# Windowed attention and spatial gating on one core: q and k transposed by identity products into f32 PSUM, batch 0 as a software pipeline, Ln directly behind its product, turns a batch ahead

## The chip, the cores and the metric

The kernel runs on one core of one Trainium2 chip. The metric is the device time of one launch in microseconds. A kernel is run several times; the text gives medians with the lowest and highest run. A run more than 1.5% above the fastest of the same kernel counts as slow, and comparisons use fast runs alone.

Names of engines in the profile: PE is TensorE, PEld its weight loads, DVE is VectorE, ACT is ScalarE, POOL is GpSimd, SP is SyncE. A "q" behind a name (ACTq) is that engine's sequencer, for instance where it issues a DMA.

## The reference

There are 8 batches of 8 heads, 576 positions and head size 64. The attention is causal with a window of 64 positions; its output goes through a gated block that mixes positions.

```python
scores = q @ k.T / sqrt(64);  mask = (0 <= rel) & (rel < 64)
attn   = softmax(where(mask, scores, -1e9));  x = attn @ v        # -> [8, 576, 512]
h = maximum(x @ w_in, 0);  u, v = h[..., :512], h[..., 512:]
v_n = (v - mean(v)) / sqrt(var(v) + 1e-6)
v_s = einsum('ts,bsd->btd', w_spatial, v_n) + b_spatial[None, :, None]
out = (u * v_s) @ w_out
```

All inputs and the output are f32 in memory; the kernel computes in f16 with f32 sums.

## The kernel before

Per batch the kernel treats five "pairs" `s`: four pairs of heads over the first 512 positions, and a fifth for the last 64 positions of all heads. A pair goes through T (transpose q and k), S (scores), E (Exp and mask), P (product with v and the row sums), N (normalise, giving x). The gated block of a batch consists of units V, L, U, G, O (products with w_in, the normalisation, the spatial product, w_out). The attention of batch a+1 is woven between the units of batch a.

Batches 0 to 3 (`NPE = 4`) transpose on PE. Each partition of a loaded tile holds four consecutive positions (`"(p t) d -> p (t d)"`, t=4), so the transposes come out sorted by t, and the copy home must interleave them: it writes every fourth f16.

```python
def emit_T(b, s):                                   # s < 4 shown
    tp = psp.tile([128, 1024], f16, tag="mm", bufs=4, ...)
    for y, x in enumerate("kq"):
        w = NH[b, x][:, 512 * s:512 * s + 512].rearrange("p (t n) -> p t n", t=4)
        for t in range(4):
            nc.tensor.transpose(tp[:, n * y + 128 * t:n * y + 128 * t + 128], w[:, t, :], id16[:, :])
    for y, x in enumerate("kq"):
        o = TR[b, x][:, :].rearrange("p (a n) -> p a n", a=4)
        nc.vector.tensor_copy(o[:, s, 0:512].rearrange("p (n t) -> p t n", t=4),
                              tp[:, n * y:n * y + n].rearrange("p (t n) -> p t n", t=4))
```

P writes the PSUM tile `oz`, of which there is only one buffer. N is in two halves: Ln of the row sums, then Exp of minus that and the multiply into x, which reads `oz` too. So the next P cannot start before x of the pair ahead is done.

```python
oz = psp.tile([128, 2, 512], f32, tag="oz", bufs=1, ...)              # in emit_P
# emit_N1: lnz = Ln(oz[:, 1])                       ScalarE
# emit_N2: zinv = Exp(-lnz)                         ScalarE
#          x = oz[:, 0] * zinv                      VectorE

def att(i, s):
    for f in state["post"]: f()
    post = []
    if s < 5:
        emit_S(i, s); emit_E(i, s)
    if state["P"] is not None:
        pb, ps_ = state["P"]
        emit_P(pb, ps_)
        post += [lambda: emit_N1(pb, ps_), lambda: emit_N2(pb, ps_)]
    state["P"] = (i, s) if s < 5 else None
    state["post"] = post
# run(a, seq): after every gated unit (V, U, G, O, L, W, Q):
#     if state["post"]: state["post"].pop(0)()
```

One entry of `post` is emitted after each following unit. Ln therefore stands behind the output of one unit and Exp and multiply behind the output of a second one. A unit O ends in a copy of its result on ScalarE and a store, which ScalarE issues for the first three batches:

```python
ob = mpool.tile([128, 512], f32, tag="ob", bufs=3, ...)
nc.scalar.copy(ob[:, :], po[:, :])
(nc.scalar if b < 3 else nc.sync).dma_start(out[b, 128 * j:128 * j + jn, :], ob[p0:p0 + jn, :])
```

Batch 0 has no batch ahead of it to weave into, and goes pair by pair, with matmuls on scratch data (`warm`) that are meant to keep PE's clock up:

```python
for s in range(4):
    ...                                             # casts of pair s+1, v, weights
    att(0, s)
    warm(4)
    emit_T(0, s + 1)
    warm(2)
```

The softmax here doesn't subtract the row's maximum and nothing guards it: scores larger than these inputs give would overflow.

## Time and profile before

| | before |
|---|---|
| time | 280.72 us (279.23 to 282.01, 3 runs) |
| span of the profiled run, granted clock | 280.1 us, 0.92 |
| busy PE / DVE / ACT | 80% / 64% / 54% |
| last x of batch 0, 1, 2, 3 ends at | 36.0, 77.0, 114.1, 149.2 us |
| copies of transposed k and q, 16 each | 1291 and 1337 ns |

The page of the profile gives busy time per engine, and below it the busy share of the 16 DMA engines in 40 equal slices of the span (a digit of 9 is 90% or more):

```profile
...
PE 223.3 (80%) x2733; PEld 118.7 (42%) x2733; DVE 178.1 (64%) x329; ACT 151.7 (54%) x272; POOL 110.1 (39%) x157
...
DMA  7999999999896903979031002899289922002104
...
```

No engine is full over the whole span. The DMA engines are close to full for about the first 80 us, in which batches 0 to 3 are loaded. From the groups of instructions (line, engine, operation, tiles, shapes, count, then busy us and mean ns, then idle time before them and what ended it):

```profile
...
L398 DVE TENSOR_TENSOR x<-oz,zi 128x512 f16<-128x512 f32 (+1 forms) x40 | 25.2, 631 | 39.9 <-ACT zi L396 39.6 <-issue 0.3
...
L268 DVE COPY tq<-tp 128x512 f16<-128x512 f16 x16 | 21.4, 1337 | 0.0
L268 DVE COPY tk<-tp 128x512 f16<-128x512 f16 x16 | 20.7, 1291 | 7.2 <-PE tp L258 7.2
...
```

The copies of line 268 take about twice as long as the multiply of line 398 (685 ns for its 128x512 form alone; the 631 above mixes in a smaller form), although both read and write 512 elements per partition. From the waits (engine, line and what it waited for, then us in total, times, longest):

```profile
...
PE oz L370 <- DVE x L398: 26.4, 22, 3.1
...
PE sc L286 <- DVE tq L268: 16.2, 8, 5.0
...
```

PE waits 26.4 us for x to free `oz`, and 16.2 us for the copies before it can start scores. The chain of waits that ended last, in order of time (start, duration, what), for one pair of batch 1:

```profile
...
60.24 1.83 PE po L528 x4
...
62.09 0.59 ACT ob L531
...
62.71 0.35 ACTq L441
...
63.11 0.60 ACT ln L388
63.71 0.48 ACT ob L531
...
64.22 0.34 ACTq L441
...
64.60 0.64 ACT zi L396
...
65.26 0.70 DVE x L398
...
66.00 0.64 PE oz L370 x2
...
```

This is the code of `att` and `run` at work. P has ended at 60.24; then come product, copy and store issue of a unit O (62.09, 62.71), and only then Ln (63.11); then copy and store of the next unit (63.71, 64.22), and only then Exp (64.60), the multiply on DVE (65.26), and the next P at 66.00. The same view for one transpose of batch 2:

```profile
...
90.59 0.46 PE tp L258 x8
...
91.08 1.31 DVE tk L268
```

Eight transposes take 0.46 us, 0.057 us apart; the copy behind them takes 1.31 us.

### The profile page before, as it was taken

To read this page: it belongs to the slowest core of one execution; us is meant where nothing else is said; L and a number is where in the kernel's file an instruction comes from. 1 tells how busy PE (TensorE), PEld (TensorE's weight loads), DVE (VectorE), ACT (ScalarE), POOL (GpSimd) and SP (SyncE) were. 2 spreads that over 40 slices of the span, in tenths; PEclk is the share of its full clock that TensorE was granted. 3 is DMA by queue.
4 is the path that set the end of the run, shared out by engine and by line. 5 is a ranking of instruction groups with operands and counts; after the bars stand their busy time and mean duration, and the time that the engine had idled before them with its cause. 6 is when DMAs were issued, how large, how long until landed. Compare 5 with 4: busy or idle time off the path is not lost.

```text
span 280.1 us, 6696 instructions
## 1 busy us (share of the span) xinstructions
PE 223.3 (80%) x2733; PEld 118.7 (42%) x2733; DVE 178.1 (64%) x329; ACT 151.7 (54%) x272; POOL 110.1 (39%) x157
## 2 busy tenths in 40 slices
PE   7367998975775875877969877979797979797994
PEld 2234435633333552434524543534453545353451
DVE  5865467982378970698808873765576657662750
ACT  2353554344562744575445864775477547755823
POOL 3683686008920089200980494036902680000000
PEclk9977797977797998899989997997999899999999
DMA  7999999999896903979031002899289922002104
GB/s 204 251 228 229 239 192 267 207 263 277 181 195 143 160 2 107 257 142 170 3 129 41 3 5 80 193 194 192 98 196 194 200 89 81 21 2 112 59 0 169
DMA packets 77647, 40.43 MB, mean 144 GB/s; under 512 B 44272, under 2 KB 73008, under 8 KB 77616
## 3 DMA queue, kind: packets, MB, share of 16 engines
q1 hardware_dynamic: 73424, 34.22, 58.1%
q0 software_dynamic: 2224, 2.24, 4.7%
q10 hardware_dynamic: 1968, 3.54, 3.8%
q8 instruction: 21, 0.34, 0.6%
q14 instruction: 10, 0.08, 0.1%
HBM read 32.79 MB, written 9.44 MB: 151 GB/s over the span
## 4 chain that ended last, share of the span: by engine, by line
PE 47%; DVE 35%; ACT 12%; issue 4%; ACTq 1%; POOL 0%; POOLq 0%
PE ps L509 9%; PE pv L422 8%; PE po L528 8%; DVE x L398 6%; DVE tq L268 5%; DVE tk L268 5%; PE oz L370 5%; DVE vn L479 4%; DVE st L431 4%; DVE g L512 4%; PE pu L489 3%; PE oz L380 3%; DVE e L354 3%; ACT e L344 3%; ACT zi L396 2%
## 5 line engine op out<-in xcount | busy, mean ns | idle before, releaser
L171 POOL CAST nk<-fk 128x512 f16<-128x512 f32 (+2 forms) x23 | 19.2, 835 | 101.8 <-PE tp L263 61.7
L344 ACT ACTIVATE e<-sc 128x1024 f16<-128x1024 f32 x32 | 32.8, 1026 | 41.5 <-PE sc L286 23.6
L398 DVE TENSOR_TENSOR x<-oz,zi 128x512 f16<-128x512 f32 (+1 forms) x40 | 25.2, 631 | 39.9 <-ACT zi L396 39.6
L171 POOL COPY vs<-vn 64x512 f16<-64x512 f16 (+1 forms) x56 | 43.5, 776 | 3.1
L509 PE MATMUL ps<-wspT,vn 128*128 128x512 f16 (+1 forms) x160 | 40.2, 401 | 0.0
L531 ACT COPY ob<-po 128x512 f32<-128x512 f32 x32 | 18.8, 586 | 34.6 <-PE po L528 34.1
L431 DVE BATCH_NORM_STATS2 st<-vs 128x6 f32<-128x512 f16 (+1 forms) x40 | 27.0, 674 | 14.7 <-ACT vs L429 14.7
L354 DVE TENSOR_TENSOR e<-e,mask 128x1024 f16<-128x1024 f16 x32 | 25.8, 806 | 15.6 <-ACT e L344 15.5
L422 PE MATMUL pv<-win,x 128*128 128x512 f16 (+1 forms) x132 | 34.9, 412 | 0.0
L528 PE MATMUL po<-wout,g 128*128 128x512 f16 x128 | 34.7, 420 | 0.0
L489 PE MATMUL pu<-x,win 128*128 128x512 f16 x128 | 30.8, 391 | 0.0
L171 POOL CAST vn<-vf 128x512 f16<-128x512 f32 (+1 forms) x40 | 25.3, 640 | 10.9 <-DMA vf<-in_v_dram 10.1
L429 ACT ACTIVATE vs<-pv 128x512 f16<-128x512 f32 (+1 forms) x40 | 22.9, 597 | 8.2 <-PE pv L422 5.8
L388 ACT ACTIVATE ln<-oz 128x512 f32<-128x512 f32 (+1 forms) x40 | 22.1, 554 | 9.1 <-PE oz L380 6.6
L370 PE MATMUL oz<-e,onesK 128*64 128x512 f16 x64 | 14.2, 431 | 16.1 <-DVE x L398 15.8
L512 DVE TENSOR_TENSOR g<-ps,ru 128x512 f16<-128x512 f32 x32 | 21.6, 686 | 8.3 <-PE ps L509 8.1
L268 DVE COPY tk<-tp 128x512 f16<-128x512 f16 x16 | 20.7, 1291 | 7.2 <-PE tp L258 7.2
L396 ACT ACTIVATE zi<-ln 128x512 f32<-128x512 f32 (+1 forms) x40 | 23.5, 588 | 2.8 <-ACT ob L531 2.1
L509 PEld LDWEIGHTS <-vn 128*128 128x128 f16 (+1 forms) x160 | 15.3, 103 | 17.7 <-issue 3.7
L268 DVE COPY tq<-tp 128x512 f16<-128x512 f16 x16 | 21.4, 1337 | 0.0
L370 PEld LDWEIGHTS <-onesK 128*64 128x64 f16 x80 | 7.0, 109 | 31.3 <-issue 28.6
L171 POOL CAST nq<-fq 128x512 f16<-128x512 f32 (+2 forms) x23 | 18.7, 815 | 3.9 <-DMA fq<-in_q_dram 3.9
(82 smaller groups left out, 326.9 us busy)
## 6 DMA issues: line engine op xcount, KB each, us to landing
vf<-in_v_dram SPq DMA_DIRECT2D x40, 128.0 KB, 5.5
out_dram<-ob SPq DMA_DIRECT2D x20, 256.0 KB, 2.0
fk<-in_k_dram SPq DMA_DIRECT2D x32, 144.0 KB, 3.7
fq<-in_q_dram SPq DMA_DIRECT2D x32, 144.0 KB, 4.5
fk<-in_k_dram SPq DMA_DIRECT2D x16, 256.0 KB, 5.7
fq<-in_q_dram SPq DMA_DIRECT2D x16, 256.0 KB, 5.4
vf<-in_v_dram SPq DMA_DIRECT2D x16, 256.0 KB, 6.0
out_dram<-ob ACTq DMA_DIRECT2D x12, 256.0 KB, 2.8
```

The costliest lines, as they stand in the source:

```text
L171: nc.gpsimd.tensor_copy(o, i)
L268: nc.vector.tensor_copy(o[:, s, 0:512].rearrange("p (n t) -> p t n", t=4), tp[:, n * y:n * y + n].rearrange("p (t n) -> p t n", t=4))
L344: nc.scalar.activation(e2[:, :, :], sc[0][:, :, :], AF.Exp, bias=0.0, scale=0.125)
L354: nc.vector.tensor_tensor(e2[:, :, :], e2[:, :, :], m, ALU.min)
L370: nc.tensor.matmul(oz[64 * h:64 * h + 64, 1, 0:n], onesK[:, :], e2[:, h, 0:n], start=True, stop=True)
L398: nc.vector.tensor_tensor(x[:, 0:n], oz[:, 0, 0:n], zinv[:, 0:n], ALU.mult)
L422: nc.tensor.matmul(PV[b, j][0:jn, :], xcol(b, r, j), w_in_sb[:, r, 512:1024], start=(r == 0), stop=(r == 3))
L431: nc.vector.bn_stats(st6[0:jn, 0:6], vs[0:jn, :])
L489: nc.tensor.matmul(pu[:, :], w_in_sb[:, r, 128 * m:128 * m + 128], X[b, r][:, :], start=(r == 0), stop=(r == 3))
L509: nc.tensor.matmul(ps[:, :], VN[b, kk][0:kn, 128 * m:128 * m + 128], wspT[kk][0:kn, 0:512], start=(kk == 0), stop=(kk == 4))
L512: nc.vector.tensor_tensor(g[:, :], ps[:, :], ru[:, :], ALU.mult)
L528: nc.tensor.matmul(po[:, :], G[b, r][:, 128 * j:128 * j + 128], w_out_sb[:, r, :], start=(r == 0), stop=(r == 3))
```

## The change

The change does five things.

- (a) The four transposes of a pair become products with the identity into an f32 PSUM tile, and are written there with a stride of four elements, so that they lie in token order. The copy home becomes a contiguous cast. In batch 0 the copy of q goes to ScalarE.
- (b) Batch 0 becomes a software pipeline: mask and normalisation of earlier pairs stand between T and S of a pair; the casts of q go to POOL; two warm matmuls per pair disappear. The casts of a pair get a tile each.
- (c) Ln is emitted directly behind P, Exp and multiply behind the next unit.
- (d) Batches 5 to 7, which are turned by 32x32 blocks on DVE, are turned a batch ahead (`R` in place of `T`).
- (e) The casts on POOL are emitted a batch earlier, and the order of units changes a little.

```diff
-    def emit_T(b, s):
-        tp = psp.tile([128, 1024], f16, tag="mm", bufs=4, name=f"tp{b}_{s}")
+    def T_mm(b, s):
+            tp = [psp.tile([128, 512], f32, tag="mm", bufs=4, name=f"tp{b}_{s}{x}") for x in "kq"]
...
+                    o = tp[y][:, :].rearrange("p (n t) -> p t n", t=4)
                     for t in range(4):
-                        nc.tensor.transpose(tp[:, n * y + 128 * t:n * y + 128 * t + 128],
-                                            w[:, t, :], id16[:, :])
+                        nc.tensor.matmul(o[:, t, :], w[:, 128 * t:128 * t + 128], id16[:, :],
+                                         start=True, stop=True)
...
+    def T_out(b, s):
-                nc.vector.tensor_copy(o[:, s, 0:512].rearrange("p (n t) -> p t n", t=4),
-                                      tp[:, n * y:n * y + n].rearrange("p (t n) -> p t n", t=4))
+                (act_copy if b == 0 and y == 1 else dve_copy)(o[:, y, s, 0:512], tp[y][:, :])
...
@@ att @@
             emit_P(pb, ps_)
-            post += [lambda: emit_N1(pb, ps_), lambda: emit_N2(pb, ps_)]
+            emit_N1(pb, ps_)
+            post.append(lambda: emit_N2(pb, ps_))
...
@@ batch 0; emit_E split into E_exp and E_mask, emit_N2 into N_exp and N_mul @@
-    for s in range(4):
-        ...
-        att(0, s)
-        warm(4)
-        emit_T(0, s + 1)
-        warm(2)
+    for s in (0, 1, 2, 4, 3):
+        pairs_in(0, s, dve_copy, pool_copy if s != 3 else dve_copy)
+        if s == 4:
+            emit_T(0, 4)
+            continue
+        ...
+        T_mm(0, s)
+        if s > 0:
+            E_mask(0, s - 1)
+        if s > 1:
+            N_mul(0, s - 2)
+        T_out(0, s)
+        emit_S(0, s)
+        E_exp(0, s)
+        if s > 0:
+            emit_P(0, s - 1)
+            emit_N1(0, s - 1)
+            N_exp(0, s - 1)
         warm(4)
...
@@ batches 1 to 7: orders of units; two of the four @@
-            run(a, "V0 V1 V2 T0 V3 Q L U0 U1 A0 U2 T1 U3 U4 A1 G0 G1 A2 G2 G3 A3 G4 A4 O0 O1 O2 A5 O3")
+            run(a, "V0 V1 V2 V3 Q L T0 U0 U1 T1 A0 U2 U3 A1 U4 G0 G1 A2 G2 G3 A3 G4 O0 A4 R0 O1 O2 "
+                   "A5 R1 O3")
-            run(a, "T0 V0 V1 V2 A0 V3 Q A1 L U0 T1 U1 U2 U3 A2 U4 G0 G1 A3 G2 G3 G4 A4 O0 O1 O2 A5 O3")
+            run(a, "V0 V1 A0 V2 V3 Q A1 L U0 U1 U2 A2 U3 U4 G0 A3 G1 G2 G3 A4 G4 R0 O0 O1 A5 O2 R1 O3")
```

More of the change, by code (lines that the diff above doesn't have):

```diff
@@ L52 @@
     TR = {}
+    XI = {"k": 0, "q": 1}
     VF = {}
@@ L63, in new_qkv @@
             NF[b, x] = inpool.tile([128, 2560], f32, tag=f"f{x}", bufs=2, name=f"f{x}{b}")
-            NH[b, x] = inpool.tile([128, 2560], f16, tag=f"n{x}", bufs=1, name=f"n{x}{b}")
-            TR[b, x] = apool.tile([128, 2304], f16, tag=f"t{x}", bufs=2, name=f"t{x}{b}")
+            if b < NPE:
+                for s in range(5):
+                    NH[b, x, s] = inpool.tile([128, 512], f16, tag=f"n{x}{s}", bufs=1,
+                                              name=f"n{x}{s}_{b}")
+            else:
+                NH[b, x] = inpool.tile([128, 2304], f16, tag=f"n{x}", bufs=1, name=f"n{x}{b}")
+        TR[b] = apool.tile([128, 2, 2304], f16, tag="tr", bufs=2, name=f"tr{b}")
         VF[b] = inpool.tile([128, 5, 8, 64], f32, tag="vf", bufs=2, name=f"vf{b}")
@@ L84, in cast_four @@
         if s < 4:
-            copy(NH[b, x][:, 512 * s:512 * s + 512].rearrange("p (t h d) -> p h t d", t=4, h=2),
+            copy(NH[b, x, s][:, :].rearrange("p (t h d) -> p h t d", t=4, h=2),
                  NF[b, x][:, 512 * s:512 * s + 512].rearrange("p (h t d) -> p h t d", t=4, h=2))
         else:
-            copy(NH[b, x][0:64, 2048:2560], NF[b, x][0:64, 2048:2560])
+            copy(NH[b, x, 4][0:64, :], NF[b, x][0:64, 2048:2560])
     def load_pairs(b):
@@ L138, in turn @@
     def turn(b, x, hp):
-        o = TR[b, x][:, 1152 * hp:1152 * hp + 1152].bitcast(u32)
+        o = TR[b][:, XI[x], 1152 * hp:1152 * hp + 1152].bitcast(u32)
         n = NH[b, x][:, 1152 * hp:1152 * hp + 1152].bitcast(u32)
@@ L248 @@
     SC = {}
-    def emit_T(b, s):
-        tp = psp.tile([128, 1024], f16, tag="mm", bufs=4, name=f"tp{b}_{s}")
-        n = 512 if s < 4 else 256
+    TP = {}
+    def T_mm(b, s):
+        if s < 4:
+            tp = [psp.tile([128, 512], f32, tag="mm", bufs=4, name=f"tp{b}_{s}{x}") for x in "kq"]
+        else:
+            tp = psp.tile([128, 512], f16, tag="mm", bufs=4, name=f"tp{b}_{s}")
+        TP[b, s] = tp
         with nc.named_scope(f"T{b}_{s}"):
             for y, x in enumerate("kq"):
+                w = NH[b, x, s]
@@ L255, in emit_T @@
                 if s < 4:
-                    w = NH[b, x][:, 512 * s:512 * s + 512].rearrange("p (t n) -> p t n", t=4)
+                    o = tp[y][:, :].rearrange("p (n t) -> p t n", t=4)
                     for t in range(4):
-                        nc.tensor.transpose(tp[:, n * y + 128 * t:n * y + 128 * t + 128],
-                                            w[:, t, :], id16[:, :])
+                        nc.tensor.matmul(o[:, t, :], w[:, 128 * t:128 * t + 128], id16[:, :],
+                                         start=True, stop=True)
@@ L260, in emit_T @@
                 else:
-                    w = rest(NH[b, x])
                     for p in range(4):
-                        nc.tensor.transpose(tp[:, n * y + 64 * p:n * y + 64 * p + 64],
-                                            w[:, 2 * p:2 * p + 2, :], id16[0:64, 0:64])
-        for y, x in enumerate("kq"):
-            o = TR[b, x][:, :].rearrange("p (a n) -> p a n", a=4)
+                        nc.tensor.transpose(tp[:, 256 * y + 64 * p:256 * y + 64 * p + 64],
+                                            w[0:64, 128 * p:128 * p + 128], id16[0:64, 0:64])
@@ L267, in emit_T @@
+    def T_out(b, s):
+        tp = TP.pop((b, s))
+        o = TR[b][:, :, :].rearrange("p x (a n) -> p x a n", a=4)
+        for y in (0, 1):
             if s < 4:
-                nc.vector.tensor_copy(o[:, s, 0:512].rearrange("p (n t) -> p t n", t=4),
-                                      tp[:, n * y:n * y + n].rearrange("p (t n) -> p t n", t=4))
-            else:
-                nc.vector.tensor_copy(o[:, :, 512:576],
-                                      tp[:, n * y:n * y + n].rearrange("p (a n) -> p a n", a=4))
+                (act_copy if b == 0 and y == 1 else dve_copy)(o[:, y, s, 0:512], tp[y][:, :])
+            else:
+                nc.vector.tensor_copy(o[:, y, :, 512:576],
+                                      tp[:, 256 * y:256 * y + 256].rearrange("p (a n) -> p a n", a=4))
@@ L274, in emit_S_pe, with emit_T @@
+    def emit_T(b, s):
+        T_mm(b, s)
+        T_out(b, s)
     def emit_S_pe(b, s):
@@ L276, in emit_S_pe @@
         SC[b, s] = [sc]
-        K, Q = (TR[b, x][:, :].rearrange("p (a n) -> p a n", a=4) for x in "kq")
+        K, Q = (TR[b][:, y, :].rearrange("p (a n) -> p a n", a=4) for y in (0, 1))
         with nc.named_scope(f"S{b}_{s}"):
@@ L300, in scores @@
         rows = slice(32 * g, 32 * g + 32)
-        K, Q = (TR[b, x][:, :].rearrange("p (a n e) -> p a n e", a=2, e=2) for x in "kq")
+        K, Q = (TR[b][:, y, :].rearrange("p (a n e) -> p a n e", a=2, e=2) for y in (0, 1))
         return [lambda e=e: nc.tensor.matmul(
@@ L338, in emit_S, with E_exp @@
                             t[e]()
-    def emit_E(b, s):
+    def E_exp(b, s):
         sc = SC.pop((b, s))
@@ L344, in emit_E @@
             nc.scalar.activation(e2[:, :, :], sc[0][:, :, :], AF.Exp, bias=0.0, scale=0.125)
-            m = mask[:, :, :, :].rearrange("p h u w -> p h (u w)")
         else:
@@ L352, in emit_E, with E_mask @@
             nc.scalar.activation(e2[:, :, 0:n], sc[0][:, :, 0:n], AF.Exp, bias=0.0, scale=0.125)
+        E2[b, s] = e2
+    def E_mask(b, s):
+        e2 = E2[b, s]
+        if s < 4:
+            m = mask[:, :, :, :].rearrange("p h u w -> p h (u w)")
+        else:
             m = maskr[:, :, :].rearrange("p (h u) w -> p h (u w)", h=2)
         nc.vector.tensor_tensor(e2[:, :, :], e2[:, :, :], m, ALU.min)
-        E2[b, s] = e2
+    def emit_E(b, s):
+        E_exp(b, s)
+        E_mask(b, s)
     def slot(b, r):
@@ L389, in emit_N1, with N_exp, N_mul @@
         LZ[b, s] = lnz
-    def emit_N2(b, s):
+    ZI = {}
+    def N_exp(b, s):
         n = 512 if s < 4 else 256
         lnz = LZ.pop((b, s))
-        oz = OZ.pop((b, s))
         zinv = apool.tile([128, 512], f32, tag="zinv", bufs=2, name=f"zi{b}_{s}")
         nc.scalar.activation(zinv[:, 0:n], lnz[:, 0:n], AF.Exp, bias=0.0, scale=-1.0)
+        ZI[b, s] = zinv
+    def N_mul(b, s):
+        n = 512 if s < 4 else 256
+        zinv = ZI.pop((b, s))
+        oz = OZ.pop((b, s))
         x = xpool.tile([128, n], f16, tag=f"x{s}", bufs=2, name=f"x{b}_{s}")
@@ L399, in emit_N2 @@
         X[b, s] = x
+    def emit_N2(b, s):
+        N_exp(b, s)
+        N_mul(b, s)
     def mm(name):
@@ L573, in run @@
                         turn(a + 1, x, n)
+            elif c == "R":
+                if a + 2 < B:
+                    for x in "kq":
+                        turn(a + 2, x, n)
             elif c == "F":
@@ L617, in batch_in @@
                 shift_part(b, c // 2, pool_copy)
-    pairs_in(0, 0, dve_copy, act_copy)
-    v_in(0, 0)
-    emit_T(0, 0)
-    for s in range(4):
-        v_in(0, s + 1)
-        if s == 1:
+    for s in (0, 1, 2, 4, 3):
[3 more added lines that the diff above has]
+            continue
+        v_in(0, s)
+        if s == 2:
             load_win(1)
             load_win(0)
-        if s == 3:
-            load_wsp()
-            load_wout()
-        if s == 2:
-            pairs_in(0, 4, dve_copy, act_copy)
-        if s < 3:
-            pairs_in(0, s + 1, dve_copy, act_copy)
-        att(0, s)
+        T_mm(0, s)
[10 more added lines that the diff above has]
+            N_exp(0, s - 1)
         warm(4)
-        emit_T(0, s + 1)
-        warm(2)
+    v_in(0, 4)
+    load_wsp()
+    load_wout()
     load_pairs(2)
     batch_in(1)
-    att(0, 4)
-    run(0, "p0003 p0103 F")
-    att(0, 5)
-    run(0, "p0203 p0303 F p0034 o0 p0134 o1 p0234 o2 p0334 o3 Q L U0 U1 U2 U3")
+    emit_S(0, 4)
+    E_exp(0, 4)
+    E_mask(0, 3)
+    N_mul(0, 2)
+    run(0, "p0003 p0103")
+    emit_P(0, 3)
+    emit_N1(0, 3)
+    emit_N2(0, 3)
+    E_mask(0, 4)
+    run(0, "p0203 p0303")
+    emit_P(0, 4)
+    emit_N1(0, 4)
+    emit_N2(0, 4)
+    run(0, "p0034 o0 p0134 o1 p0234 o2 p0334 o3 Q L U0 U1 U2 U3")
     run(0, "W0 W1 W2 W3 W4 U4 T0 G0 G1 T1 A0 G2 G3 T2 A1 G4 O0 T3 A2 O1 O2 T4 A3 O3")
-    run(0, "A4 p1003 p1103 F A5 p1203 p1303 F")
+    run(0, "F A4 p1003 p1103 F A5 p1203 p1303 F")
     for a in range(1, B):
@@ L656 @@
                 load_batch(a + 2)
+        if a + 2 < B and a > 1:
+            batch_in(a + 2)
         if a == 1:
@@ L659 @@
                    "G1 G2 T4 A3 G3 G4 A4 O0 O1 A5 O2 O3")
+            batch_in(3)
         elif a == 2:
-            run(a, "V0 T0 V1 V2 T1 A0 V3 Q T2 A1 L U0 U1 U2 T3 A2 U3 U4 G0 G1 T4 A3 G2 G3 G4 A4 "
-                   "O0 O1 O2 A5 O3")
+            run(a, "V0 T0 V1 T1 A0 V2 V3 Q T2 A1 L U0 U1 U2 T3 A2 U3 U4 G0 T4 A3 G1 G2 G3 A4 "
+                   "G4 O0 O1 A5 O2 O3")
         elif a == 3:
-            run(a, "V0 V1 V2 T0 V3 Q L U0 U1 A0 U2 T1 U3 U4 A1 G0 G1 A2 G2 G3 A3 G4 A4 O0 O1 O2 A5 O3")
-        else:
-            run(a, "T0 V0 V1 V2 A0 V3 Q A1 L U0 T1 U1 U2 U3 A2 U4 G0 G1 A3 G2 G3 G4 A4 O0 O1 O2 A5 O3")
-        if a + 2 < B:
-            batch_in(a + 2)
+            run(a, "V0 V1 V2 V3 Q L T0 U0 U1 T1 A0 U2 U3 A1 U4 G0 G1 A2 G2 G3 A3 G4 O0 A4 R0 O1 O2 "
+                   "A5 R1 O3")
+        else:
+            run(a, "V0 V1 A0 V2 V3 Q A1 L U0 U1 U2 A2 U3 U4 G0 A3 G1 G2 G3 A4 G4 R0 O0 O1 A5 O2 R1 O3")
     run(B, "Q")
```

## The prediction

> **What bounds it now.** No engine is full: the page gives PE 80%, DVE 64%, ACT 54% of 280.1 us. The chain that ended last (47% PE, 35% DVE, 12% ACT) changes by stage; in order of time: batch 0's attention to its last x at 36.0 us; batch 0's V and normalisation to 44.8; batch 1's attention to 77.0; batch 2's to about 112; batch 3's to 145; then 31, 28, 28 and 26.5 us per batch, and a 21.7 us tail. In the stretches PE is busy 17 to 18 of 20 us late, about 15 of 20 before 145 us. There the chain goes through DVE copies of transposed q and k (5.2% + 4.9% = 28 us), which write f16 with a stride of four: 1291 and 1337 ns for 128x512, 1.1 us apart back to back. In batch 0 score groups start at 9.1, 13.7, 19.8, 26.8, 30.9 us although pair 3's v is in at 17.0; PE meanwhile runs its warm matmuls at 0.43 us each.
>
> **What changes.**
> 1. The stride moves from the DVE write to the PE write. The copy becomes contiguous f32 PSUM to f16. The Trainium skill (VectorE: DVE Perf Modes, "Why PSUM operands drop a tier") gives f32 from PSUM the 1x mode; the trace's f32-PSUM multiplies (685 ns, 0.6 apart) agree. Estimate 0.65 us, 0.58 apart: 32 copies save about 0.5 us of pitch each, four of batch 0 also go to ACT. About 18 us of DVE, 11 to 13 of it on the chain.
> 2. Identity products now write PSUM with a 16-byte stride. The Trainium skill (PSUM, "Specifications (TRN2)") says non-contiguous patterns slow matmuls significantly; no run here shows it yet. If halved in speed, 8 products of a pair go from 0.43 to 0.86 us: 7 us of PE in all, some 3 on the chain.
> 3. Batch 0 pipeline: mask and normalise of the previous pairs run between transpose and scores, q casts go to POOL, two warm matmuls per pair disappear. Scores of pair 3 come at about 20.5 instead of 26.8, x of batch 0 ends near 30.5 (the weights' arrival, issue at 14.3 plus 9.9 us, starts to bind): -5.5 us.
> 4. Ln directly behind P, no longer behind the next unit's output copy and store issue (chain at 60 to 72 us). About 1.4 us per affected step, two or three steps in batches 1 to 3: -4.
> 5. Batches 5 to 7 are turned a batch ahead, out of the chain (1.35 us per batch, PE waits of up to 2.4 us on it): about -1.5 per batch for four batches, -6.
>
> Per stage: batch 0 -5.5, batch 1 -5, batch 2 -4.5, batch 3 -3, later -5, minus 2 to 3 for the slower products: about -20 us.
>
> **Predicted 260 us, 250 to 270 for 8 in 10.** Faster by over 2%: 0.95; within 2%: 0.04; slower: 0.01.
>
> **Right if:** the copies show 0.6 to 0.7 us; DVE busy falls to about 158 us; x of batch 0 ends near 30 us; PE idle before "sc waiting for tq" (16 us) falls by half; the stretches after 145 us shorten by 1 to 2 us per batch. **Step wrong if:** identity products show over 0.3 us spacing, or PE waits for PSUM buffers behind them.
>
> **What would break it:** products slowed fourfold (+20 us of PE); DMA, full until 80 us, becoming the bound of batch 1 (its last v lands near 44 us); a lower granted clock (now 0.92) as PE gets denser; the gain of batch 0 given back waiting for w_in.

## The result, and the profile after

| | before | after |
|---|---|---|
| time | 281.37 us (279.23 to 283.40, 4 runs) | 260.98 us (258.21 to 263.23, 4 runs) |
| ratio of fast runs | | 0.920, 95% interval 0.907 to 0.933 |
| busy PE / DVE / ACT, us | 223.3 / 178.1 / 151.7 | 223.5 / 164.8 / 151.1 |
| last x of batch 0, 1, 2, 3 ends at | 36.0, 77.0, 114.1, 149.2 | 33.0, 72.1, 105.5, 132.6 |

All ratios here are the mean time of one kernel's fast runs over that of the other's fast runs of the same rounds, so not quite the ratio of the medians that stand beside them. Two of the four runs of after count as slow; its two fast ones have a mean of 258.8 us, against 281.3 of before. The profiled run of the changed kernel took 262.51 us and counts as slow (granted clock 0.93; its fast runs had 0.95 and 0.96), while that of the kernel before is fast. Readings that need exact sizes are therefore taken from the experiments, most of whose profiled runs are fast. The numerical result is correct here and in all runs below.

The page, same lines as before:

```profile
...
PE 223.5 (86%) x2725; PEld 120.6 (46%) x2725; DVE 164.8 (63%) x326; ACT 151.1 (58%) x271; POOL 115.0 (44%) x161
...
DMA  6999999999997903877086003899499932004105
...
```

PE does the same amount of work in a shorter span. The groups, for pair 2 (VectorE does k, and q except in batch 0; ScalarE does q of batch 0):

```profile
...
L180 DVE CAST tr<-tp_2k 128x512 f16<-128x512 f32 x4 | 2.7, 675 | 1.9 <-PE tp_2k L270 1.9
...
L180 DVE CAST tr<-tp_2q 128x512 f16<-128x512 f32 x3 | 2.0, 678 | 0.0
...
L183 ACT CAST tr<-tp_2q 128x512 f16<-128x512 f32 x1 | 0.6, 585 | 0.2 <-PE tp_2q L270 0.2
...
```

The contiguous copy takes 0.68 us on DVE in place of 1.29 to 1.34, and 0.59 us on ScalarE. The waits:

```profile
...
PE oz L396 <- DVE x L431: 15.8, 11, 3.1
...
PE sc L303 <- DVE tr L180: 6.2, 5, 2.3
...
```

Both waits of PE have shrunk, by 10.6 and 10.0 us. Identity products in the chain of waits, batch 2:

```profile
...
86.22 0.44 PE tp_2k L270 x4
86.65 0.44 PE tp_2q L270 x4
...
```

Four products now take 0.44 us, so 0.11 us apart: exactly half the speed of the transposes before. Finally, the timeline of ScalarE around the first stores of batch 0 (start, duration, instruction; in brackets how long it was idle before and what ended that):

```profile
...
52.22 0.59 ACT L414 ACTIVATE ln<-oz 128x512 f32<-128x512 f32 x1
52.84 0.63 ACT L423 ACTIVATE zi<-ln 128x512 f32<-128x512 f32 x1
53.45 0.58 ACT L568 COPY ob<-po 128x512 f32<-128x512 f32 x1
55.84 0.39 ACTq L478 DMA_DIRECT2D out_dram<-ob  x1
56.33 1.02 ACT L361 ACTIVATE e<-sc 128x1024 f16<-128x1024 f32 x1 [2.30 <-PE po L565]
...
```

Ln and Exp now stand together, and the copy `ob` has ended by 54.03. But its store is issued at 55.84, and ScalarE stood still for 1.8 us in between. This wait is new: in the kernel before, the first store was issued 0.03 us after its copy.

### The profile page after: what moved, and what is told of

It is laid out like the page before. It is cut to its first block, busy times and chain, and to the rows that moved or that the text cites. A ratio compares the mean times of both kernels' runs of the same rounds, so it can differ in the third digit from the quotient of the medians.

```text
span 260.8 us, 6702 instructions
## 1 busy us (share of the span) xinstructions
PE 223.5 (86%) x2725; PEld 120.6 (46%) x2725; DVE 164.8 (63%) x326; ACT 151.1 (58%) x271; POOL 115.0 (44%) x161
## 4 chain that ended last, share of the span: by engine, by line
PE 47%; SPq 17%; DVE 16%; ACT 9%; DMA 7%; issue 3%; ACTq 1%
PE ps L546 11%; PE pv L459 7%; PE po L565 7%; SPq L122 7%; SPq L83 7%; PE pu L526 6%; DMA vf<-in_v_dram 5%; DVE vn L516 5%; DVE st L468 4%; PE oz L396 3%; PE sc L319 3%; SPq L87 3%; DVE x L431 2%; PE oz L406 2%; ACT e L361 2%
## 5 line engine op out<-in xcount | busy, mean ns | idle before, releaser
L177 POOL COPY vs<-vn 64x512 f16<-64x512 f16 (+1 forms) x56 | 44.5, 794 | 3.1
L377 DVE TENSOR_TENSOR e<-e,mask 128x1024 f16<-128x1024 f16 x32 | 27.8, 868 | 21.3 <-ACT e L361 21.0
L546 PE MATMUL ps<-wspT,vn 128*128 128x512 f16 (+1 forms) x160 | 39.3, 394 | 0.0
L526 PE MATMUL pu<-x,win 128*128 128x512 f16 x128 | 34.3, 418 | 0.0
L565 PE MATMUL po<-wout,g 128*128 128x512 f16 x128 | 31.1, 385 | 0.0
L177 POOL CAST vn<-vf 128x512 f16<-128x512 f32 (+1 forms) x40 | 26.9, 682 | 9.1 <-DMA vf<-in_v_dram 8.3
L177 POOL CAST nq<-fq 128x512 f16<-128x512 f32 (+2 forms) x27 | 21.3, 790 | 12.8 <-DMA fq<-in_q_dram 10.9
L546 PEld LDWEIGHTS <-vn 128*128 128x128 f16 (+1 forms) x160 | 15.2, 102 | 16.7 <-issue 1.9
L528 ACT ACTIVATE ru<-pu 128x512 f32<-128x512 f32 x32 | 17.2, 593 | 6.0 <-PE pu L526 6.0
L459 PEld LDWEIGHTS <-x 128*128 128x128 f16 (+1 forms) x132 | 12.8, 104 | 16.1 <-issue 3.2
L526 PEld LDWEIGHTS <-win 128*128 128x128 f16 x128 | 12.2, 105 | 16.0 <-issue 5.5
```

The lines of the kernel that those rows point to most:

```text
L177: nc.gpsimd.tensor_copy(o, i)
L377: nc.vector.tensor_tensor(e2[:, :, :], e2[:, :, :], m, ALU.min)
L459: nc.tensor.matmul(PV[b, j][0:jn, :], xcol(b, r, j), w_in_sb[:, r, 512:1024], start=(r == 0), stop=(r == 3))
L526: nc.tensor.matmul(pu[:, :], w_in_sb[:, r, 128 * m:128 * m + 128], X[b, r][:, :], start=(r == 0), stop=(r == 3))
L546: nc.tensor.matmul(ps[:, :], VN[b, kk][0:kn, 128 * m:128 * m + 128], wspT[kk][0:kn, 0:512], start=(kk == 0), stop=(kk == 4))
L565: nc.tensor.matmul(po[:, :], G[b, r][:, 128 * j:128 * j + 128], w_out_sb[:, r, :], start=(r == 0), stop=(r == 3))
```

## The experiments

Twelve kernels were run in three calls, each beside its own runs of the kernel before (medians 281.26, 281.65 and 283.27 us; these differ between calls, so the ratios carry the comparison). A difference in us given below is one between means of fast runs; across calls it can be off by a us or two. "T" below is the new transposes with their copies, "N" is Ln directly behind P, "the pipeline" is batch 0's new order, "the turns" is the new unit orders with turns and casts a batch ahead.

| run | what it is | median us (range) | mean of fast runs (number) | ratio to before, 95% |
|---|---|---|---|---|
| after | T, N, pipeline, turns | 260.98 (258.21–263.23) | 258.8 (2) | 0.920 [0.907, 0.933] |
| only_T | before + T | 273.08 (272.40–273.15) | 272.9 (4) | 0.973 [0.969, 0.978] |
| only_TN | before + T + N | 259.59 (257.97–262.59) | 259.1 (3) | 0.915 [0.908, 0.922] |
| undo_T | after without T | 269.89 (269.68–270.72) | 270.0 (4) | 0.963 [0.958, 0.968] |
| read_stride | after, stride on the read of the copy | 260.80 (260.46–267.08) | 260.7 (3) | 0.929 [0.924, 0.935] |
| undo_N | after without N | 275.46 (274.49–276.73) | 275.5 (4) | 0.974 [0.966, 0.982] |
| undo_pipe | after without the pipeline | 258.54 (256.53–260.59) | 257.9 (3) | 0.918 [0.909, 0.926] |
| undo_turn | after without the turns | 263.01 (261.06–264.92) | 263.0 (4) | 0.931 [0.923, 0.939] |
| store_sp | after, all stores from SyncE | 252.05 (251.01–253.82) | 252.2 (4) | 0.893 [0.885, 0.901] |
| undo_N_store_sp | store_sp without N | 264.32 (263.06–267.90) | 263.9 (3) | 0.934 [0.926, 0.942] |
| oldpipe_store_sp | store_sp without the pipeline | 250.52 (248.85–254.54) | 250.0 (3) | 0.885 [0.877, 0.893] |
| store_sp_warm | store_sp + 8 warm matmuls | 250.54 (248.21–253.55) | 248.5 (2) | 0.878 [0.871, 0.885] |
| best | oldpipe_store_sp + read_stride | 252.60 (251.15–253.81) | 252.5 (4) | 0.892 [0.886, 0.899] |

The theory after the result was that T is worth what was predicted, and that the other parts add up as predicted. The rivals were that one of them carries nearly all of the rest, and that some gain of batch 0 is lost again in batch 1.

### only_T: the new transposes alone

```diff
@@ emit_T of before @@
-        tp = psp.tile([128, 1024], f16, ...)
+            tp = [psp.tile([128, 512], f32, tag="mm", bufs=4, name=f"tp{b}_{s}{x}") for x in "kq"]
...
-                        nc.tensor.transpose(tp[:, n * y + 128 * t:...], w[:, t, :], id16[:, :])
+                        nc.tensor.matmul(o[:, t, :], w[:, t, :], id16[:, :], start=True, stop=True)
...
-                nc.vector.tensor_copy(o[:, s, 0:512].rearrange("p (n t) -> p t n", t=4), ...)
+                nc.vector.tensor_copy(o[:, s, 0:512], tp[y][:, :])
```

> The kernel before with the transposes alone changed (f32 products written with a 16-byte stride, contiguous copies on VectorE), every order as before. Theory of the prediction: copies 0.68 instead of 1.3 us save 11 to 13 us on the chain and the slower products give 3 back, so about 272 us (ratio 0.965 to 0.975). Rival (the new orders make the gain, the stride only moves work from VectorE to TensorE): 278 us or more, ratio 0.99 or above.

Measured: 273.08 us; by fast runs 7.6 us below before. This is close to the 8 to 10 us that steps 1 and 2 of the prediction give together. The timeline of ScalarE shows the new wait at the store here already, and longer:

```profile
...
52.25 0.59 ACT L533 COPY ob<-po 128x512 f32<-128x512 f32 x1 [0.63 <-PE po L530]
56.82 0.45 ACTq L443 DMA_DIRECT2D out_dram<-ob  x1
57.33 0.63 ACT L398 ACTIVATE zi<-ln 128x512 f32<-128x512 f32 x1 [4.49 <-DMA fq<-in_q_dram]
...
```

The copy ended at 52.84 and the store was issued at 56.82, 4.0 us later. Exp of the pair, emitted behind the store, started only at 57.33, after 4.5 us in which ScalarE did nothing.

### undo_T and read_stride: which side of the copy minds the stride

```diff
@@ undo_T: after, with transposes into f16 PSUM, contiguous, and the copy of before @@
+        tp = psp.tile([128, 1024], f16, tag="mm", bufs=4, name=f"tp{b}_{s}")
+                        nc.tensor.transpose(tp[:, 512 * y + 128 * t:512 * y + 128 * t + 128], ...)
+                src = tp[:, 512 * y:512 * y + 512].rearrange("p (t n) -> p t n", t=4)
+                dst = o[:, y, s, 0:512].rearrange("p (n t) -> p t n", t=4)    # strided write
@@ read_stride: the same, but the elements are walked in the order of the destination @@
+                src = tp[:, 512 * y:512 * y + 512].rearrange("p (t n) -> p n t", t=4)  # strided read
+                dst = o[:, y, s, 0:512].rearrange("p (n t) -> p n t", t=4)    # contiguous write
```

> The changed kernel with only the transposes put back (f16 transposes into one PSUM buffer, copies that write with a stride), all new orders kept. If the stride's move is worth 8 to 10 us and parts add up: 269 to 271 us. If the new orders make nearly all of the gain: 262 us or less.

> The changed kernel with f16 transposes written without a stride into one PSUM buffer and the stride put on the read of the copy, whose write is contiguous; the result stays right. Products should come back to 0.055 us apart (0.11 in the changed kernel) and hold one PSUM buffer of four. If a strided 16-bit PSUM read runs near 1 element per cycle (0.65 to 0.7 us per copy) and the slow products cost 3 us of the chain: 257 to 258 us. If the slow products are hidden: no difference from the changed kernel (within 1 us). If strided reads are as slow as strided writes (1.3 us): 268 us or more, like undo_T.

Both kernels copy the same elements from the same f16 PSUM tile to the same place. The groups of undo_T:

```profile
...
L180 DVE COPY tr<-tp 128x512 f16<-128x512 f16 x28 | 34.2, 1312 | 5.6 <-PE tp L266 5.6
...
L183 ACT COPY tr<-tp 128x512 f16<-128x512 f16 x4 | 5.2, 1297 | 16.9 <-DVE tr L180 16.9
...
```

and of read_stride:

```profile
...
L180 DVE COPY tr<-tp 128x512 f16<-128x512 f16 x28 | 17.9, 676 | 5.5 <-PE tp L266 5.5
...
L183 ACT COPY tr<-tp 128x512 f16<-128x512 f16 x4 | 2.3, 586 | 13.8 <-DVE tr L180 13.8
...
```

With the stride of 8 bytes on the write the copy takes 1.31 us on DVE and 1.30 us on ScalarE; with a stride of 256 bytes on the read and a contiguous write 0.68 and 0.59 us. So it was the strided write that cost a factor of two, on both engines, and neither the f16 PSUM source nor the stride as such. undo_T is slower than after by 11 us (the ratios, 0.963 against 0.920, would make it 12). That may not be the worth of T alone: in undo_T's profile the granted clock is 0.50 from 14 to 38 us and the last x of batch 0 comes at 43.0 us, against 33.0 in after, whose clock is down only from about 21 to 28 us. Whether the longer copies brought that fall about or it came by chance was not separated. The cleaner size of T is the 7.6 us of only_T.

read_stride also gives the transposes their full speed back (0.057 us apart), and its time is not shown to differ from that of after (260.7 and 258.8 us by fast runs, intervals overlapping). The "3 us on the chain" that the prediction charged for slower products do not show. The intervals are wide, though, and read_stride's clock was 0.50 from 18 to 30 us in its profile, so a us or two can't be excluded.

### only_TN and undo_N: Ln directly behind P

```diff
@@ only_TN: only_T with @@
-            post += [lambda: emit_N1(pb, ps_), lambda: emit_N2(pb, ps_)]
+            emit_N1(pb, ps_)
+            post.append(lambda: emit_N2(pb, ps_))
@@ undo_N: after with the same lines the other way round @@
```

> The changed kernel with the Ln of the softmax sums put back behind the next unit (as before), all else new. The prediction gave the earlier Ln 4 us: then 264 to 265 us (ratio to the kernel before 0.94). Rival: ScalarE has room, the Ln was rarely the last wait: within 1 us of the changed kernel (ratio 0.92).

> The kernel before with two parts alone: the new transposes and the Ln directly behind P; batch 0's order, unit orders and turns as before. only_T measured 273. If these two make the whole gain (the pipeline of batch 0 measured nothing, the turns 2.5 us): 260 to 263 us, ratio 0.925 to 0.935. If the Ln pays only together with the new unit orders: 268 us or more.

Two lines are worth 15 to 17 us here: undo_N takes 275.5 us, after 258.8 (ratios 0.974 and 0.920). Going the other way, only_TN takes 259.1 where only_T takes 272.9, 13.9 us less. And only_TN, with neither pipeline nor turns, is as fast as the whole change (0.915 and 0.920, intervals overlapping). The prediction had 4 us for this step. The wait of PE for x, first in only_T:

```profile
...
PE oz L372 <- DVE x L400: 30.8, 24, 5.3
...
```

and in only_TN:

```profile
...
PE oz L372 <- DVE x L400: 13.9, 16, 3.6
...
```

The wait fell by 16.9 us, about as much as the time. It fell not only at two or three steps of batches 1 to 3: in only_T PE waited for x 24 times, in only_TN 16 times and shorter. Cut at the last x of each batch, the fall is 1.5 us in batch 0, 4.0, 2.7 and 2.0 in batches 1 to 3, 2.3 in batch 4 and 4.5 after it.

### undo_N_store_sp: N measured without the disturbance at the stores

> store_sp (252 us) with the Ln put back behind the next unit. undo_N cost 14 us against the changed kernel; its trace shows ScalarE blocked 7.4 us at the first store with Ln and Exp of the softmax behind it. If the blocked store made the Ln's size: 256 to 258 us here (4 to 6 us over store_sp). If the Ln is on the chain by itself in batches 1 to 4: 262 us or more (over 10 us over store_sp).

It is store_sp (below) with the two lines of undo_N. The question was whether N's worth is an artefact of ScalarE standing still at the stores, because undo_N stands still the longest of the kernels looked at (7.4 us at its first store). With the stores on SyncE, N is still worth 11.7 us: 263.9 against 252.2, or 0.934 against 0.893. The waits of undo_N_store_sp:

```profile
...
PE oz L396 <- DVE x L431: 22.4, 22, 2.3
...
```

and of store_sp:

```profile
...
PE oz L396 <- DVE x L431: 10.9, 10, 2.0
...
```

The 11.5 us between them account for that difference. One pair of batch 1 in the chain of waits of undo_N_store_sp shows how a step is longer:

```profile
...
54.82 0.41 PE oz L396 x2
...
55.48 0.98 PE po L565 x4
...
56.48 0.59 ACT ob L568
57.07 0.50 ACT ln L414
...
57.92 0.66 ACT zi L423
...
58.61 0.70 DVE x L431
...
59.35 0.41 PE oz L396 x2
...
```

From one P (54.82) to the next (59.35) are 4.53 us: P, the product of a unit O, its copy, and only then Ln, Exp and multiply. In store_sp the same pair's P starts at 54.17 and the next at 57.73, 3.56 us later. Its ScalarE timeline:

```profile
...
55.22 0.59 ACT L414 ACTIVATE ln<-oz 128x512 f32<-128x512 f32 x1
55.84 0.59 ACT L568 COPY ob<-po 128x512 f32<-128x512 f32 x1
56.32 0.63 ACT L423 ACTIVATE zi<-ln 128x512 f32<-128x512 f32 x1
...
```

Ln runs at 55.22 beside the unit's product, and only the copy stands before Exp. So a step is about 1.0 us shorter; with some twelve of them in the run this makes the 12 us. (Twelve is read from two counts: PE's waits for x fall from 22 to 10, and in the DVE timelines of only_T and only_TN twelve of the 40 multiplies of x stand at a new place in the order.)

### undo_pipe and oldpipe_store_sp: batch 0 in its old order

```diff
@@ batch 0 @@
-    for s in (0, 1, 2, 4, 3):       # the pipeline
-        ...
+    for s in range(4):              # the loop of before
+        ...
+        att(0, s)
+        warm(4)
+        emit_T(0, s + 1)
+        warm(2)
```

> The changed kernel with batch 0 emitted in the old order (q casts on ScalarE, mask and normalise behind their own pair, two more warm matmuls per pair), the rest new. The trace puts the last x of batch 0 3.0 us earlier in the changed kernel. If that gain is kept to the end: 263 to 265 us. If it is given back in batch 1, where the trace shows the DMA queues full until 75 us: 261 us or less, no difference.

> undo_pipe with the stores of batches 0 to 2 issued from SyncE. There ScalarE lost 4.6 us at the first store (50.4 to 55.1). If that wait is the loss: 253 to 255 us, the last x of batch 1 near 66 instead of 69.5 us. If not: 258 us as undo_pipe.

undo_pipe takes 257.9 us against 258.8; with the stores moved, oldpipe_store_sp 250.0 against 252.2. The intervals overlap both times. The pipeline gains nothing that could be measured; if it does anything, it costs a little. With T and N in place the old loop reaches the scores of pair 3 at 20.8 us (before 26.8) and the last x of batch 0 at 29.7, while the pipeline gets there at 22.0 and 33.0 in the profiled run of after. only_TN, which has the old loop too, is there at 20.5 and 28.7. The start of pair 3's scores in PE's timeline, before:

```profile
...
26.84 0.42 PE L286 MATMUL sc<-tq,tk 64*64 64x128 f16 x16 [1.67 <-DVE tq L268]
...
```

in only_TN:

```profile
...
20.53 0.42 PE L288 MATMUL sc<-tq,tk 64*64 64x128 f16 x16 [0.51 <-DVE tq L271]
...
```

and in after:

```profile
...
22.04 0.64 PE L303 MATMUL sc<-tr 64*64 64x128 f16 x16 [1.59 <-DVE tr L180]
...
```

What the pipeline was to gain, T and N had already gained in the old loop.

In the pipeline, cast and copies of pair 3 stand in DVE's queue with mask and multiply of the pairs ahead, and PE waits for them 1.2 us before the identity products of pair 3 and 1.6 us before its scores (timeline of PE in after). This brings in the clock.

### store_sp_warm: the clock in batch 0

```diff
@@ store_sp, batch 0's pipeline @@
             emit_T(0, 4)
+            warm(4)
             continue
...
         T_mm(0, s)
+        if s == 3:
+            warm(4)
```

> store_sp with 4 warm matmuls in each of two TensorE pauses of batch 0 (behind the transposes of the rest and of pair 3). In the profiles the last x of batch 0 comes at 29.6 us where the granted clock stays 1.0 from 20 to 30 us and at 32.4 to 36.2 us where it falls to half. If the pauses cause the fall: clock 1.0 there, last x near 29.6 us, about 249 us. If not: 252 us as store_sp.

The busy time and clock of the stretch from 20 to 25 us (us of the stretch, then busy us of each engine, then the granted clock, the DMA share and GB/s), in after:

```profile
...
20.00:25.00 5.00, 3.41 (x42) 1.73 (x40) 2.71 (x4) 2.80 (x4) 4.54 (x8) 0.59 1.19 224
...
```

and in store_sp_warm:

```profile
...
20.00:25.00 5.00, 3.53 (x60) 1.75 (x60) 2.65 (x3) 2.63 (x4) 4.87 (x9) 1.00 1.20 223
...
```

The granted clock in this stretch is 0.59 in after (0.54 in store_sp) and 1.00 with eight more scratch matmuls. The last x of batch 0 comes at 30.4 in place of 32.6 us, and that of batch 1 at 65.6 in place of 66.7. undo_N supports this from the other side: it has exactly after's code for batch 0, happened to keep its clock at 1.00, and reached the scores of pair 3 at 20.3 and the end of batch 0 at 29.6. So about 2 to 3 us of the pipeline's lateness is the clock. With the clock kept, the pipeline stands where the prediction put it (20.5 and 30.5); the old loop simply gets there too.

The Trainium skill (TensorE: Matmul & The Clock Gate, "What's actually happening") says that the clock halves after an idle window of about 3.4 us, that the window runs freely, and that the transition therefore varies; the clocks of 0.5 to 0.6 against 1.0 on the same code agree with the variation. No pause of 3.4 us shows in this trace: before the fall in after PE pauses for 1.2 and 1.6 us, and from 18.0 to 21.4 us it is busy for 1.2 us (2.1 in undo_N and 2.8 in store_sp_warm, which kept their clock). How much idling it takes was not measured.

In total, store_sp_warm takes 248.5 us by its two fast runs, against 252.2 of store_sp. The intervals of the ratios just touch (0.871 to 0.885 and 0.885 to 0.901), and the runs come from different calls, so a gain of some 4 us, near the 249 us expected, is likely but not settled. Nor is batch 0 its whole cause: of the 2.2 us there 1.1 is left at the end of batch 1, and the granted clock of the whole profiled run is also higher (0.979 against 0.946).

### store_sp: all stores from SyncE

```diff
-        (nc.scalar if b < 3 else nc.sync).dma_start(out[b, 128 * j:128 * j + jn, :],
+        nc.sync.dma_start(out[b, 128 * j:128 * j + jn, :],
```

> The changed kernel with the stores of batches 0 to 2 issued from SyncE instead of ScalarE. Theory: in batch 1 ScalarE stands still because a store cannot be issued while the load queues are full (in the trace the first store waits 1.8 us in the changed kernel, 4.0 in only_T, 4.6 in undo_pipe, and 0.03 in the kernel before, always until 55 to 57 us), so batch 0's gain is given back there. Then ScalarE's wait at the stores goes, the last x of batch 1 comes 3 us or more earlier and the time falls to 256 to 258 us. Rival: batch 1 waits for the loaded data or the clock itself: no change, or slower because the loads of batch 3 queue behind the stores.

252.05 us; by fast runs 6.6 us below after (the ratios, 0.893 and 0.920, would make it 7.6), the largest gain of any single edit to the changed kernel. Last x of batch 1 comes at 66.7 in place of 72.1 us. ScalarE's waits before its store issues add up to 4.3 us in after (1.8, 0.85, 0.5 and 0.84 at the first four, 0.03 at each later one) and to 0.4 us in before.

The expectation blamed a DMA queue full of loads. That theory fell on reading the built program. All DMAs that SyncE and ScalarE issue take one of eight completion counters in turn, and before a counter is used again the program waits until the DMA that used it last has landed. The wait stands on the engine that issues. For the first store of batch 0 in after, ScalarE's list of instructions holds a wait for the counter last used by a load of batch 2's k, pair 3. The waits of undo_N name a load of k as what ScalarE waited for there:

```profile
...
ACT zi L423 <- DMA fk<-in_k_dram: 8.6, 2, 7.8
...
```

The trace of after has that load issued at 50.60 with 5.2 us to landing, which gives 55.8; the store was issued at 55.84. In undo_N the same load was issued at 50.09 and took 5.7 us, which gives 55.8, and the store, whose data had been ready at 48.47, was issued at 55.84. So ScalarE waits for a load that has nothing to do with it, and how long depends on how early the store comes: in the kernel before, batch 0 was so late that the load had landed.

This shows the wait and what ends it. It does not account for all of the 6.6 to 7.6 us. The measured waits make 4.3 us, and the end of batch 1 moved by 5.3 (in profiles of which that of after is a slow run). Moving the stores also moves the loads: SyncE now issues four stores at 53.67 to 60.48 us and the loads of batch 3 start only then, at 60.58 in place of 53.74. Whether fewer loads beside batch 1 add to the gain was not separated.

### undo_turn: the old orders for batches 1 to 7

```diff
-        if a + 2 < B and a > 1:
-            batch_in(a + 2)
...                                        # the four unit orders of before, turns T0 T1 in place of R0 R1
+        if a + 2 < B:
+            batch_in(a + 2)               # behind run(), as before
```

> The changed kernel with the unit orders of batches 1 to 7, the turns of batches 4 to 7 and the places of their casts put back as before. The prediction gave this 5 to 6 us, from batch 3 on: then 266 us. Rival: those batches are bound by TensorE and its granted clock, whatever the order: within 1.5 us of the changed kernel.

263.0 us against 258.8, ratios 0.931 and 0.920, with overlapping intervals. The turns and earlier casts are worth some 3 to 4 us at most and perhaps nothing: only_TN does without them and is not slower. The prediction had 6.

### best: everything that had looked good

> The parts that paid, together: old order of batch 0, stores from SyncE, stride on the read of the copy (f16 transposes, one PSUM buffer), the rest as changed. oldpipe_store_sp measured 250.5; the read stride measured no difference from the write stride of the products (260.8). Expected 249 to 251 us; under 249 if the freed TensorE time and PSUM buffer count once the store no longer blocks.

252.5 us; oldpipe_store_sp without the strided read had 250.0 in another call, with overlapping intervals. The strided read gains nothing again, and the run does not deserve its name. The fastest kernels measured are store_sp_warm and oldpipe_store_sp, at 248.5 and 250.0 us, 11 to 12% below before. They are not told apart.

## Why the prediction was right, and where it was right by luck

The predicted time, 260 us, was met at 260.98 (258.8 by fast runs). Its steps were not all met: two terms were too large and one too small, and they cancelled. That part was luck.

| step of the prediction | predicted, us | measured, us |
|---|---|---|
| 1 and 2: stride moves, products slower | -8 to -10 | -7.6 (only_T); -11 to -12 (undo_T, with a halved clock in batch 0) |
| 3: pipeline of batch 0 | -5.5 | none measurable (undo_pipe, oldpipe_store_sp) |
| 4: Ln behind P | -4 | -13.9, -16.7, -11.7 (only_TN, undo_N, undo_N_store_sp) |
| 5: turns a batch ahead | -6 | 0 to -4 (undo_turn, only_TN) |
| sum | -23.5 to -25.5 | -22.5 |

The prediction's own total of -20 is not the sum of its steps but of its list of stages; where the rest went it does not say. The stages were met no better. From one last x to the next, batch 0 gained 3.0 us (predicted 5.5), batch 1 1.9 (5), batch 2 3.7 (4.5), batch 3 8.0 (3) and all that follows 2.7 (5), 19.3 us together in the profiled runs, of which that of after is a slow one.

**The stride (step 1) was right.** The estimate of 0.65 us per copy met 0.67 to 0.68. The Trainium skill (VectorE: DVE Perf Modes, "Why PSUM operands drop a tier") gives f32 from PSUM the 1x mode; 512 elements at 0.68 us beside f32-PSUM multiplies at 0.69 agree, but do not test it: the f16 copies of read_stride took 0.68 us too. The wait of scores for copies fell from 16.2 to 6.2 us, by more than the half that was asked for. DVE's busy time fell only to 164.8 us, not 158. Part of the miss is other work: the mask of line 377 took 27.8 us in place of 25.8 and the normalisation of line 516 17.2 in place of 15.0, in the same number of instructions.

**The slower products (step 2) were right in rate and are not shown to be on the chain.** They run at exactly half speed, 0.11 against 0.057 us. The Trainium skill (PSUM — Partial Sum Buffer, "Specifications (TRN2)") says only that non-contiguous patterns slow matmuls significantly; for a stride of 16 bytes this is a factor of two. The predicted 3 us on the chain did not show: read_stride has the fast transposes and no shorter time. Of the two signs against this step, the spacing stayed below 0.3 us, and the other came once: PE waited 1.5 us for a PSUM buffer before the identity products of one k (tp_1k, for ACT's ru).

**The pipeline (step 3) is the step that failed.** The prediction took the chain of before through batch 0, with copies of 1.3 us and Ln late, and credited the pipeline with shortening it. But steps 1 and 4 shorten the same stretch: only_TN, with the old loop, has the scores of pair 3 at 20.5 us, exactly where the prediction put the pipeline, and ends batch 0 at 28.7, earlier than after (33.0 us, where the prediction had 30.5; 29.6 with the same code and a full clock in undo_N). The gain was credited to the wrong edit. What the prediction had listed among its dangers, that batch 0's gain might be given back, did occur too, but not by waiting for w_in: ScalarE's stores wait for counters of loads, 1.8 us at the first store in after and up to 7.4 in undo_N, against 0.03 in before and 0.02 in undo_T, whose batch 0 ended latest: the earlier the store is ready, the longer the wait.

**Ln behind P (step 4) was right in mechanism and mis-sized in number.** The prediction read one example (60 to 66 us of before), put 1.4 us on it, and guessed two or three affected steps. A clean pair shows 1.0 us per step (4.53 against 3.56), and there were about twelve of them. `oz` has one buffer, so no P can start before x of the pair ahead; the line "PE oz waits for DVE x, 26.4 us, 22 times" of before had said so, and the prediction did not use its count.

**The turns (step 5) were too large.** The prediction took PE's waits of up to 2.4 us on the turns, four batches of 1.5 us, as gain. At most 3 to 4 us of it shows, and within the noise of the runs. The sign that the prediction had named for it did appear: from the last x of batch 3 to that of batch 7 before took 112.0 us and after 107.1, 1.2 us less per batch. But only_TN, without the turns, needs 106.8 for it, so the sign does not tell for the turns. Nor was all of it kept: from that x to the end took 18.9 us before and 21.1 after.

**The dangers.** DMA is still full up to about 75 us and did hold up batch 1, through the counters. The granted clock did not fall in total (0.93 to 0.96 in after, 0.92 in the profiled run of before), but it halved inside batch 0.

## What to carry to other kernels

Count how often a wait occurs before sizing its removal: a single PSUM buffer between two engines can make each of its uses a step of the chain, and moving one instruction ahead of an unrelated unit was worth more here than a new pipeline. When several edits shorten the same stretch, their gains do not add; measure one alone before crediting the next. Put the interleaving on the side of a copy that costs nothing measurable, here the read, and do not let a computing engine issue a DMA whose completion counter is shared with loads in flight.

## What the Trainium skill lacked or had wrong

- SBUF — State Buffer, "Specifications (TRN2)", asks for two or more hits per 16-byte line for full bandwidth, and adds that each step to a new line costs. Two hits were not enough here: the f16 copy that wrote every fourth element, two per 16 bytes, took 1.31 us on DVE and 1.30 us on ScalarE; with a contiguous write 0.68 and 0.59 us (undo_T and read_stride). That row does not say whether it is for reads or writes.
- PSUM — Partial Sum Buffer, "Specifications (TRN2)", has no figure for the slowdown of matmuls that write with a stride. With 16 bytes between f32 elements it is a factor of two: 0.11 against 0.057 us per product of 128x128.
- None of the pages consulted gives the cost of a strided read from PSUM by DVE or ScalarE: f16 with a stride of 256 bytes took 676 and 586 ns for 512 elements, as long as contiguous f32 (0.68 and 0.585 us).
- DMA: Bandwidth & Descriptors, "Issuing engines are not separate DMA queues", says that issuing from several engines saves only the sequencer's time. That section does not warn that, as in this program, the issuing engine may have to wait first for a completion counter that an earlier, unrelated DMA used: ScalarE stood still for 1.8 to 7.4 us in front of one store, until a load of 5.2 to 5.7 us had landed.
